# Turning the first rows at full depth, and ScalarE as the issuer of three of the last stores

## The chip, the cores and the metric

The kernel runs on one core of one Trainium2 chip. The metric is device time in microseconds (us), the median of several executions. A core has five engines with an instruction stream each: PE (TensorE, matrix products), DVE (VectorE), ACT (ScalarE), POOL (GpSimd) and SP (SyncE, which here only issues DMAs). Engines wait for each other through semaphores. Sixteen DMA engines move data between the chip's main memory (HBM) and the on-chip memory SBUF; results of PE land in PSUM, eight banks that DVE and ACT read.

## The reference

Attention with a few extra keys in front, then a gated feed-forward network, all in float32 outside:

```
B, H, S, Nb, D = 8, 8, 576, 16, 64        # batches, heads, rows, beacon keys, head size
k_all = concat(beacon_k, k);  v_all = concat(beacon_v, v)          # 592 keys
scores = q @ k_all.T / 8;  causal mask on the 576 keys, beacons always seen
a = softmax(scores);  attn = a @ v_all                             # (8, 8, 576, 64)
x = attn with heads side by side                                   # (4608, 512)
out = (relu(x @ w_gate) * (x @ w_val)) @ w_out                     # 512 -> 1536 -> 512
```

The output is 4608 x 512 float32.

## The kernel before

**The work.** Attention goes batch by batch. For each batch, `new_batch` loads q, k and v with DMAs on SP into staging tiles `st` (seven of 128 x 512 float32), rounds them to bfloat16 tiles `h16` (three buffers `cast_s`; the function `rounded`, line 486, on POOL and for some of batch 0 on DVE), and turns them on PE: `turned` (line 490) multiplies the rounded rows with an identity matrix, so that head dimension comes to the partitions. There are ten turns per batch, of four matmuls each: four for k and four for q (128 rows, `load_pair`), and two from `load_rest`. Of these, "first" ("F" in the orders of loading) holds 48 rows of q and 16 beacon keys, 64 rows in all, and "last" ("L") holds 64 rows of k and 16 of q, 80 rows. In a turn, `h16` is the stationary operand (loaded into PE as weights) and the identity the moving one; the number of partitions that both take is the depth of the multiplication. DVE and ACT copy what was turned from PSUM to `kT` (keys) and `diag` (queries, block-diagonal for two heads). Then follow scores on PE (lines 655 to 663), masking and row minimum on DVE (678), the exponential on ACT (689), normalisation on POOL (710), transposes of the probabilities by DMA (by PE in batch 0), and the product with v on PE (766 and 795), which gives `xT`.

**The feed-forward part.** `hidden` forms gate and value products for up to 512 rows of `xT` at a time (line 833), with relu on ACT (837) and the product of both on DVE (841). `project` multiplies 128 rows with w_out (line 853), copies the result to one of four tiles `osb` on ACT or DVE, and stores it with a DMA on SP (line 865). Of each batch, 512 rows are done so. The last 64 rows of each batch are gathered over four batches, 256 rows at a time, so that a tile of 128 rows belongs to two batches and takes two stores of 64 rows. The second gathering (batches 4 to 7) is the last work of the kernel: one tile with 512 columns, then one tile in two halves of 256 columns (`LAST_PARTS`). That makes six stores of 64 rows at the very end.

**What sets the order.** All work is first given to `Plan` as tasks with an engine (or a choice of engines), a cost, dependencies, buffers and a priority. `Plan.order` simulates the engines with these costs and writes out one order of tasks; the instructions are emitted in it and each engine's stream is fixed by it. A "DMA" task is an issue on SP. A task that has "ACT" as its engine stands in ACT's stream among the copies and activations there. PE's stream mixes attention of coming batches with feed-forward work of earlier ones, so that feed-forward matmuls fill PE while the softmax of another batch is under way.

Of the kernel before, what the change touches and what calls it, by code (L numbers as in the profile page):

```python
# [51 lines left out]
OUT = -1300.0  # L52
# [93 lines left out]
class Plan:  # L146
# [7 lines left out]
    def add(self, engines, cost, run, deps=(), holds=(), prio=0.0, lag=None, part=False, lazy=0.0, after=0.0, move=0.0):  # L154
        t = Task(engines if isinstance(engines, tuple) else (engines,), cost, run, deps, holds, prio, lag, part, lazy, move)
        t.ready = after
        for d in t.deps:
            d.users.append(t)
        self.tasks.append(t)
        return t  # L160
# [107 lines left out]
def kernel(  # L268
# [12 lines left out]
    nc = tc.nc  # L281
    B, H, S, D = q.shape
# [4 lines left out]
    P = 128  # L287
# [31 lines left out]
    ident = cp.tile([P, P], BF16, name="ident")  # L319
# [33 lines left out]
    add = plan.add  # L353


    def c_dve(n):
        return 0.07 + 0.00104 * n
# [7 lines left out]
    def c_act(n):  # L365
        return 0.06 + 0.00083 * n
# [4 lines left out]
    def c_pe(n):  # L371
        return 0.003 + n / 2400.0
# [63 lines left out]
    def copy(e, dst, src):  # L436
        if e == "ACT":
            nc.scalar.copy(dst, src)  # L438
        elif e == "DVE":
            nc.vector.tensor_copy(dst, src)  # L440
        else:
            nc.gpsimd.tensor_scalar(dst, src, 1.0, 1.0, ALU.mult, ALU.mult)
# [25 lines left out]
    def new_batch(b, prio, work):  # L468
# [20 lines left out]

        def turned(h16, rows, ca, prio, users):  # L490
            ps = Hold(first_ps if b == 0 else v_ps, 1 + users)

            def turn(_):
                for a in range(4):

                    to = ps.tile[:, a * P:a * P + rows]
                    nc.tensor.matmul(to, h16.tile[:rows, a * P:(a + 1) * P], ident[:rows, :rows],  # L497
                                     start=True, stop=True)

            return ps, add("PE", c_pe(4 * rows), turn, (ca, on_ident), (h16, ps), prio[1])  # L500
# [13 lines left out]
        def load_pair(kind, p, prio):  # L514
# [12 lines left out]
            halves = 1 if kind == "k" else 2  # L527
            zeros = on_zeros.get(b) if kind == "q" else None
            ps, tu = turned(h16, P, ca, prio, halves)

            def evict(x):
# [18 lines left out]
        def load_rest(kind, prio):  # L550
# [15 lines left out]
            i = 0 if kind == "first" else 1  # L566
            h16, ca = rounded((t.kT, t.diag), st, rows, scales[:rows, i:i + 1], prio, ld, lambda t_: t_)
            ps, tu = turned(h16, rows, ca, prio, 3)

            def evict_k(x):  # L570
# [251 lines left out]
    def hidden(rhs, w, c0, deps, hT, prio):  # L822
        hid = []
        for nf in range(NF):
            psg, psv, g = Hold(f_s, 2), Hold(f_s, 2), Hold(gate_s, 2)

            def product(w_r, ps, nf=nf):
                for ki in range(KM):
                    x = rhs(ki)
                    to = ps.tile[:, :w]  # L830
                    if len(x.shape) == 3:
                        to = to.rearrange("p (b s) -> p b s", b=x.shape[1])
                    nc.tensor.matmul(to, w_r[:, ki, nf * P:(nf + 1) * P], x, start=(ki == 0), stop=(ki == KM - 1))  # L833

            a = add("PE", 4 * c_pe(w), lambda _, f=product, ps=psg: f(wg_r, ps), deps + [weight_in["g", nf // 4]],
                    (psg,), prio + 0.02 * nf)
            r = add("ACT", c_act(w), lambda _, psg=psg, g=g: nc.scalar.activation(  # L837
                g.tile[:, :w], psg.tile[:, :w], AF.Relu), (a,), (psg, g), -1000 + prio)
            b_ = add("PE", 4 * c_pe(w), lambda _, f=product, ps=psv: f(wv_r, ps), [a, weight_in["v", nf // 4]],
                     (psv,), prio + 0.02 * nf + 0.01)  # L840
            hid.append(add("DVE", c_dve(w), lambda _, psv=psv, g=g, nf=nf: nc.vector.tensor_mul(  # L841
                hT[nf].tile[:, c0:c0 + w], g.tile[:, :w], psv.tile[:, :w]), (r, b_), (psv, g, hT[nf]), -1000 + prio))
        return hid

    def project(t0, rows, here, hT, prio, last):
        w = DM // LAST_PARTS if last else DM
        for n0 in range(0, DM, w):
            ps, osb = Hold(f_s, 4), Hold(osb_s, 1 + len(rows))
            prev = None
            for part in range(3):  # L850
                def outp(_, part=part, ps=ps, n0=n0):
                    for nf in range(4 * part, 4 * part + 4):
                        nc.tensor.matmul(ps.tile[:, :w], hT[nf].tile[:, t0:t0 + P], wo_r[:, nf, n0:n0 + w],  # L853
                                         start=(nf == 0), stop=(nf == NF - 1))

                need = [prev, weight_in["o", part]]
                for hid in here:
                    need += hid[4 * part:4 * part + 4] + (hid[:11] if part == 0 else [])
                prev = add("PE", 4 * c_pe(w), outp, need, (ps,) + tuple(hT[4 * part:4 * part + 4]),
                           prio + 0.3 + 0.01 * part + 0.001 * (n0 > 0) - (0.5 if part else 0))  # L860
            ev = add(("ACT", "DVE"), {"ACT": c_act(w), "DVE": c_dve(w)}, lambda x, ps=ps, osb=osb: copy(
                x.engine, osb.tile[:, :w], ps.tile[:, :w]), (prev,), (ps, osb), -1000 + prio)
            at = 0
            for r0, n in rows:
                add("DMA", (0.4, 0.78 * n / P), lambda _, osb=osb, r0=r0, n=n, at=at, n0=n0: nc.sync.dma_start(
                    out[r0:r0 + n, n0:n0 + w], osb.tile[at:at + n, :w]), (ev,), (osb,), prio + OUT)
                at += n


# [13 lines left out]
    def done(b, lo, hi):  # L883
        return [x for (b0, what, _), x in x_done.items() if b0 == b and SPAN[what][0] < hi and SPAN[what][1] > lo]

    REG = S // MT * MT
    for b in range(B):
        hT = [Hold(hid_s, len(CUTS.get(b, ())) + 1 + REG // P) for _ in range(NF)]
        cuts = [0, *CUTS.get(b, ()), REG]
        prio = 1000 + 10.0 * b  # L890
        here = []
        for a, z in zip(cuts, cuts[1:]):
            here.append(hidden(lambda ki, a=a, z=z, b=b: xT[:, ki, b * S + a:b * S + z], z - a, a, done(b, a, z), hT, prio))
            for t0 in range(a // P * P, z // P * P, P):
                project(t0, [(b * S + t0, P)], [x for x, c0, c1 in zip(here, cuts, cuts[1:]) if c0 < t0 + P and c1 > t0],
                        hT, prio, False)
            prio += 2.0
    ends = xT.rearrange("p k (b s) -> p k b s", s=S)
    for i in range(2):
        b0, b1 = i * B // 2, (i + 1) * B // 2  # L900
        w = (b1 - b0) * (S - REG)
        prio = 1000 + 10.0 * b1 - 5.0
        hT = [Hold(hid_s, 1 + w // P + (LAST_PARTS - 1) * i) for _ in range(NF)]
        deps = [x for b in range(b0, b1) for x in done(b, REG, S)]
        hid = hidden(lambda ki, b0=b0, b1=b1: ends[:, ki, b0:b1, REG:], w, 0, deps, hT, prio)
        for t0 in range(0, w, P):
            b = b0 + t0 // (S - REG)
            project(t0, [(x * S + REG, S - REG) for x in (b, b + 1)], [hid], hT, prio, i == 1 and t0 + P == w)

    def fill(n, to):  # L910
        for _ in range(n):
# [34 lines left out]
```

## Time and profile before

| | us |
|---|---|
| median of 3 runs | 409.17 (408.51 to 409.42) |
| the profiled execution | 410.43 |
| its span, first to last instruction | 408.7 |
| PE busy | 394.1 (96%) |
| DVE busy | 315.8 (77%) |
| ACT busy | 289.9 (71%) |
| POOL busy | 232.7 (57%) |
| granted PE clock, mean | 0.997 |

The profile is of one execution. Its page gives the busy time of each engine, the span in 40 slices of 10.2 us (each digit is a busy share in tenths), and the chain of work that ended last, followed back from the last instruction. From the trace behind it one can list waits by engine, and the timeline of a stretch: start, length, engine, line, operation, and the tiles written and read; consecutive instructions of one group are merged, and "x4" tells how many. "PEld" is the loading of weights into PE, which overlaps matmuls; "SPq" is the issuing of DMAs on SP. A matmul's form such as "64*128 64x64" names first the part of the array that the weights occupy (rows * columns) and then the moving operand. Durations of matmuls overlap their neighbours, so the room that one takes on PE is read from start to start.

### The profile page before, as it was taken

The page shows a single profiled execution, that of the slowest core. Times are in us where ns is not written, and L with a number is a line of the kernel's source. Part 1 is how long each engine was busy: PE and PEld are TensorE (multiplying, and loading weights), DVE is VectorE, ACT ScalarE, POOL GpSimd, SP SyncE. Part 2 cuts the span into 40 slices and gives each one's busy share as a digit, 9 for nine tenths or more (in the row PEclk, how much of TensorE's full clock was granted, in tenths as well). Part 3 has the DMA queues.
Part 4 walks back from the last instruction along what each step waited for, and adds up shares of the span by engine and source line. Part 5 has one row for each costly group of instructions (what it writes and reads, how often), then busy time and mean ns, then how long its engine had stood idle before and what let it go on. Part 6 is the DMA issues. An engine that isn't in the chain of part 4 may idle for free.

```text
span 408.7 us, 10376 instructions
## 1 busy us (share of the span) xinstructions
PE 394.1 (96%) x3276; PEld 246.8 (60%) x3311; DVE 315.8 (77%) x1159; ACT 289.9 (71%) x959; POOL 232.7 (57%) x434
## 2 busy tenths in 40 slices
PE   7899999989999999999999999999999999999994
PEld 5567867567766877555557754654554544444483
DVE  6898999889989988899998998787988544244251
ACT  6899989778888968797888799998867432033040
POOL 5899786947777667586975966875727200000000
PEclk9999999999999999999999999999999999999998
DMA  8899999999989999999999999999195730100112
GB/s 224 167 199 225 212 209 196 171 242 219 176 172 230 215 178 231 190 227 195 242 209 210 234 198 189 249 201 205 54 162 125 167 73 0 70 34 0 53 54 51
DMA packets 172616, 68.03 MB, mean 166 GB/s; under 512 B 146832, under 2 KB 168080, under 8 KB 172560
## 3 DMA queue, kind: packets, MB, share of 16 engines
q1 hardware_dynamic: 167808, 62.64, 75.5%
q0 software_dynamic: 4752, 4.72, 7.1%
q8 instruction: 26, 0.43, 0.5%
q14 instruction: 30, 0.25, 0.2%
HBM read 38.27 MB, written 9.44 MB: 117 GB/s over the span
## 4 chain that ended last, share of the span: by engine, by line
PE 84%; POOL 7%; DMA 2%; DVE 2%; ACT 2%; issue 2%; SPq 0%; POOLq 0%
PE f L833 42%; PE f L853 22%; PE f L663 7%; PE f L766 5%; PE f L497 4%; POOL xT L710 2%; POOL pb L710 2%; POOL h L486 2%; PE f L655 2%; DMA st<-in_beacon_k_dram 1%; PE f L795 1%; DMA st<-in_q_dram 1%; DVE diag L440 1%; PE f L745 1%; ACT xT L689 1%
## 5 line engine op out<-in xcount | busy, mean ns | idle before, releaser
L710 POOL TENSOR_SCALAR pb<-pb,small 128x576 bf16<-128x576 bf16 (+8 forms) x224 | 121.6, 557 | 56.0 <-DVE small L703 49.0
L689 ACT ACTIVATE pb<-f,small 128x64 bf16<-128x64 f32 (+6 forms) x256 | 131.0, 524 | 18.0 <-DVE small L678 13.1
L837 ACT ACTIVATE g<-f 128x512 f32<-128x512 f32 (+3 forms) x156 | 71.9, 470 | 67.9 <-PE f L833 66.6
L678 DVE CUSTOM_DVE_ANT_0 f<-f,mask 128x128 f32<-128x128 f32 (+7 forms) x256 | 112.0, 477 | 9.4 <-PE f L663 7.2
L833 PE MATMUL f<-xT,wv_r 128*128 128x512 bf16 (+3 forms) x616 | 111.8, 313 | 0.5
L833 PE MATMUL f<-xT,wg_r 128*128 128x512 bf16 (+3 forms) x619 | 109.5, 313 | 0.3
L841 DVE TENSOR_TENSOR hT<-g,f 128x512 bf16<-128x512 f32 (+3 forms) x156 | 80.5, 520 | 37.6 <-PE f L833 34.4
L853 PE MATMUL f<-wo_r,hT 128*128 128x512 bf16 (+1 forms) x423 | 102.0, 373 | 1.0
L833 PEld LDWEIGHTS <-wg_r 128*128 128x128 bf16 x624 | 60.0, 98 | 32.3 <-issue 0.2
L833 PEld LDWEIGHTS <-wv_r 128*128 128x128 bf16 x624 | 59.4, 98 | 33.0 <-issue 0.8
L853 PEld LDWEIGHTS <-hT 128*128 128x128 bf16 x444 | 41.6, 98 | 39.1
L689 ACT ACTIVATION_READ_ACCUMULATOR pb<-f,small 128x1 f32 x256 | 53.8, 210 | 0.0
L663 PE MATMUL f<-kT,diag 128*128 128x384 bf16 (+7 forms) x255 | 46.9, 286 | 1.9 <-DVE diag L440 0.8
L678 DVE DVE_READ_ACCUMULATOR2_ANT small<- 128x1 f32 x296 | 41.6, 141 | 0.2 <-issue 0.2
L486 POOL TENSOR_SCALAR h<-st 128x512 bf16<-128x512 f32 x62 | 37.8, 614 | 7.1 <-DMA st<-in_q_dram 2.9
L440 DVE COPY osb<-f 128x512 f32<-128x512 f32 (+1 forms) x26 | 17.6, 678 | 23.2 <-PE f L853 22.7
L710 POOL TENSOR_SCALAR xT<-xT,small 128x64 bf16<-128x64 bf16 (+4 forms) x64 | 26.9, 436 | 7.7 <-ACT xT L689 4.1
L497 PE MATMUL f<-ident,h 128*128 128x128 bf16 (+2 forms) x320 | 28.1, 217 | 2.8 <-POOL h L486 2.5
L438 ACT CAST diag<-f 64x512 bf16<-64x512 f32 (+2 forms) x52 | 23.0, 442 | 9.6 <-PE f L497 4.1
L497 PEld LDWEIGHTS <-h 128*128 128x128 bf16 (+2 forms) x320 | 20.3, 98 | 15.6 <-POOL h L486 7.9
L440 DVE CAST diag<-f 64x512 bf16<-64x512 f32 (+2 forms) x44 | 26.3, 598 | 4.2 <-ACT diag L438 2.0
L663 PEld LDWEIGHTS <-diag 128*128 128x128 bf16 x256 | 20.4, 98 | 15.0 <-issue 1.5
(67 smaller groups left out, 376.7 us busy)
## 6 DMA issues: line engine op xcount, KB each, us to landing
st<-in_q_dram SPq DMA_DIRECT2D x32, 256.0 KB, 4.5
st<-in_k_dram SPq DMA_DIRECT2D x32, 256.0 KB, 5.0
out_dram<-osb SPq DMA_DIRECT2D x32, 256.0 KB, 2.6
st<-in_v_dram SPq DMA_DIRECT2D x24, 256.0 KB, 4.7
st<-in_v_dram SPq DMA_DIRECT2D x8, 224.0 KB, 4.9
wg_r<-in_moe_w_gate_dram POOLq DMA_DIRECT2D x3, 512.0 KB, 8.5
wv_r<-in_moe_w_val_dram POOLq DMA_DIRECT2D x3, 512.0 KB, 10.3
wo_r<-in_moe_w_out_dram POOLq DMA_DIRECT2D x3, 512.0 KB, 14.2
```

What stands on the lines that cost most here:

```text
L438: nc.scalar.copy(dst, src)
L440: nc.vector.tensor_copy(dst, src)
L486: (nc.gpsimd if x.engine == "POOL" else nc.vector).tensor_scalar(to, of, by, 1.0, ALU.mult, ALU.mult)
L497: nc.tensor.matmul(to, h16.tile[:rows, a * P:(a + 1) * P], ident[:rows, :rows], start=True, stop=True)
L663: nc.tensor.matmul(view(i), t.diag.tile[:, p, j * P:j * P + P], kT[:, p, :n], start=True, stop=True)
L678: nc.vector.tensor_tensor_reduce(out=view(i), in0=view(i), in1=msk, scale=1.0, scalar=small["t"][:, 0:1] if name in "EF" else 3.0e38, op0= ...
L689: nc.scalar.activation(ph.tile.rearrange("p a n -> p (a n)")[:, a:a + n], view(i), AF.Exp, bias=small["t"][:, low:low + 1], scale=-1.0, ac ...
L710: (nc.gpsimd if x.engine == "POOL" else nc.vector).tensor_scalar(one, one, small["t"][:, 8 + i:9 + i], 1.0, ALU.mult, ALU.mult)
L833: nc.tensor.matmul(to, w_r[:, ki, nf * P:(nf + 1) * P], x, start=(ki == 0), stop=(ki == KM - 1))
L837: r = add("ACT", c_act(w), lambda _, psg=psg, g=g: nc.scalar.activation(g.tile[:, :w], psg.tile[:, :w], AF.Relu), (a,), (psg, g), -1000 + ...
L841: hid.append(add("DVE", c_dve(w), lambda _, psv=psv, g=g, nf=nf: nc.vector.tensor_mul(hT[nf].tile[:, c0:c0 + w], g.tile[:, :w], psv.tile[: ...
L853: nc.tensor.matmul(ps.tile[:, :w], hT[nf].tile[:, t0:t0 + P], wo_r[:, nf, n0:n0 + w], start=(nf == 0), stop=(nf == NF - 1))
```

## The change

Two edits.

1. `turned` gives the four matmuls of a turn the full 128 partitions as depth, in every batch but the first, also when only 64 or 80 rows are wanted. The further rows of `h16` hold older values; the identity has zeros where they would count, and the output keeps its 64 or 80 columns.
2. In `project`, for the second gathering only (`final`), the second of the two stores of a tile is a task of ACT, which issues the DMA on its own queue. The first remains on SP. Of the last six stores, three are then issued by each.

The order of the instructions on PE, DVE and POOL and all their waits stay as they were. SP has three stores less at its end, ACT three more at its end, behind its last copy.

```diff
         def turned(h16, rows, ca, prio, users):
             ps = Hold(first_ps if b == 0 else v_ps, 1 + users)
+            deep = P if b else rows
 
             def turn(_):
                 for a in range(4):
 
                     to = ps.tile[:, a * P:a * P + rows]
-                    nc.tensor.matmul(to, h16.tile[:rows, a * P:(a + 1) * P], ident[:rows, :rows],
+                    nc.tensor.matmul(to, h16.tile[:deep, a * P:(a + 1) * P], ident[:deep, :rows],
                                      start=True, stop=True)
...
-    def project(t0, rows, here, hT, prio, last):
+    def project(t0, rows, here, hT, prio, last, final):
...
             for r0, n in rows:
-                add("DMA", (0.4, 0.78 * n / P), lambda _, osb=osb, r0=r0, n=n, at=at, n0=n0: nc.sync.dma_start(
-                    out[r0:r0 + n, n0:n0 + w], osb.tile[at:at + n, :w]), (ev,), (osb,), prio + OUT)
+                def store(x, osb=osb, r0=r0, n=n, at=at, n0=n0):
+                    (nc.scalar if x.engine == "ACT" else nc.sync).dma_start(out[r0:r0 + n, n0:n0 + w], osb.tile[at:at + n, :w])
+
+                if final and at:
+                    add("ACT", 0.6, store, (ev,), (osb,), prio + OUT)
+                else:
+                    add("DMA", (0.4, 0.78 * n / P), store, (ev,), (osb,), prio + OUT)
                 at += n
...
-            project(t0, [(x * S + REG, S - REG) for x in (b, b + 1)], [hid], hT, prio, i == 1 and t0 + P == w)
+            project(t0, [(x * S + REG, S - REG) for x in (b, b + 1)], [hid], hT, prio, i == 1 and t0 + P == w, i == 1)
```

More of the change, by code (lines that the diff above doesn't have):

```diff
@@ L895 @@
                 project(t0, [(b * S + t0, P)], [x for x, c0, c1 in zip(here, cuts, cuts[1:]) if c0 < t0 + P and c1 > t0],
-                        hT, prio, False)
+                        hT, prio, False, False)
             prio += 2.0
```

## The prediction

> **What bounds the kernel now.** I read the page's shares and slices first, then the chain that ended last.
>
> ```profile
> span 408.7 us, 10376 instructions
> PE 394.1 (96%) x3276; PEld 246.8 (60%) x3311; DVE 315.8 (77%) x1159; ACT 289.9 (71%) x959; POOL 232.7 (57%) x434
> PE   7899999989999999999999999999999999999994
> DMA  8899999999989999999999999999195730100112
> PE 84%; POOL 7%; DMA 2%; DVE 2%; ACT 2%; issue 2%; SPq 0%; POOLq 0%
> ```
>
> TensorE is nearly full from slice 2 to slice 39 and carries 84% of the chain; POOL carries 7%. So TensorE time saved counts, unless PE then arrives at something that POOL delivers. The list of PE's waits answers where that happens: between 36 and 125 us it has one line, and between 125 and 403.3 us none at all.
>
> ```profile
> PE f L497 <- POOL h L486: 2.3, 5, 0.7
> ```
>
> Next I read the timeline of PE around a turn of 64 rows (121 us, batch 3), one of 64 rows behind 128 rows (196 us, batch 5) and one of 80 rows behind 128 rows (189.8 us), and POOL's timeline at 121 us.
>
> ```profile
> 121.08 0.38 PE L853 MATMUL f<-wo_r,hT 128*128 128x512 bf16 x1
> 121.39 0.29 PE L497 MATMUL f<-ident,h 64*128 64x64 bf16 x4
> 121.61 1.04 PE L853 MATMUL f<-wo_r,hT 128*128 128x512 bf16 x4
> 122.59 0.40 PE L497 MATMUL f<-ident,h 128*128 128x128 bf16 x4
> 122.82 0.25 PE L663 MATMUL f<-kT,diag 128*128 128x64 bf16 x2
> ...
> 196.28 0.61 PE L497 MATMUL f<-ident,h 128*128 128x128 bf16 x8
> 196.82 0.60 PE L833 MATMUL f<-xT,wv_r 128*128 128x512 bf16 x2
> ...
> 189.78 0.53 PE L497 MATMUL f<-ident,h 128*128 128x128 bf16 x8
> 190.15 0.60 PE L833 MATMUL f<-xT,wv_r 128*128 128x512 bf16 x2
> ...
> 121.92 0.61 POOL L486 TENSOR_SCALAR h<-st 128x512 bf16<-128x512 f32 x1
> ```
>
> Starts tell more than durations here, since matmuls overlap: 121.39 − 121.08 is the room that one matmul took. Last comes the tail, in the timeline from 395 us and in the landings of the final stores.
>
> ```profile
> 401.51 0.69 DVE L440 COPY osb<-f 128x512 f32<-128x512 f32 x1 [2.97 <-PE f L853]
> 401.95 0.37 ACT L438 COPY osb<-f 128x256 f32<-128x256 f32 x1 [3.95 <-PE f L853]
> 402.23 3.71 SPq L865 DMA_DIRECT2D out_dram<-osb  x6
> 403.26 0.42 DVE L440 COPY osb<-f 128x256 f32<-128x256 f32 x1 [1.05 <-PE f L853]
> ...
> DMA to landing us min/median/max: 2.0/2.0/2.0
> ```
>
> The last result is in SBUF at 403.68, but SP works through six stores without a break from 402.23 to 405.94. The last one starts at 405.35 and lands 2.0 later at 407.4, 1.47 after its issue ends; 1.3 of closing steps follow.
>
> **The change, part 1: full depth in the turn.** It alters four matmuls for "F" (64 rows) and four for "L" (80 rows) in each of batches 1 to 7; batch 0 stays. No instruction is added, and the order on PE and every wait are the same.
>
> What 64 rows cost now. Four matmuls of 128 columns take 122.82 − 122.59 = 0.23, so 0.057 each, and by columns 0.029 for one of 64. A 512-column matmul takes about 0.216 (the 49 in a run at 356.29 take 10.74). At 121 us, the way in is 0.31 − 0.216 = 0.09 too long, and four matmuls to the next start take 0.22 where 4 × 0.029 = 0.12 would do: 0.10 on the way out. Together 0.19, with some 0.01 on the next matmul 0.20. The two pairs check it: 4 × 0.057 + 4 × 0.029 = 0.34, taken 0.54 with 64 rows: 0.20 lost. With 80 rows 4 × 0.057 + 4 × 0.036 = 0.37, taken 0.37: nothing lost. So the 80-row half of the edit is worth 0, and a 64-row visit loses 0.20. At full depth the 64 columns should keep 0.029: bounds are 0.029 and the 0.057 of the 128-column form (+0.11 a visit), and I take the first, because even 32-column matmuls at 128 rows (L795, 14 from 231.03 to 231.46) start 0.031 apart.
>
> The Trainium skill ("TensorEngine Tiling (Array Packing)", Key Properties) says that a change of tiling mode drains the array; its Performance Considerations advise 2x row tiling for a contract dimension up to 64, which speaks against this change. By the advice the narrow form would gain up to half of 0.12 per visit; the trace shows no such gain, only the 0.20 of going in and out, so by it the sum would be higher by at most 7 × 0.06 = 0.4.
>
> What reaches the end. Batch 1 (38.6 us) and batch 2 (79.1 us): the way in hides under a wait for POOL's cast (both are among the five waits above), and what the way out frees is eaten by the later waits of that list (87.7 and 91.1 us, 0.6 and 0.7 long). Batch 3: at 122.59 PE starts 0.06 after POOL's cast ended (121.92 + 0.61), and the four L853 matmuls before it were done issuing at 121.61 + 0.88 = 122.49, so PE already waits 0.10; arriving earlier gains nothing unless POOL is earlier too. Batches 4 to 7 (164.1, 196.6, 232.6, 267.5 us) meet no wait that shows: 4 × 0.20 = 0.80. Bounds: 0 if casts or scores turn out only just in time, 7 × 0.20 = 1.4 if all comes through. From 300 us only PE is busy, on feed-forward matmuls whose inputs are long ready, so what is saved by then is kept.
>
> **Part 2: ScalarE issues three of the last six stores**, the second of each pair. They stand on ACT's queue behind its last copy (done 402.32), and nothing stands behind them, so they delay no compute; on SP, the first store of the next pair moves up. SP's stores now take 0.55 to 0.59 each. After: SP starts at 402.23, about 402.8, and the third when DVE's copy is done, 403.71 (the first one started 0.03 after its copy). ACT starts at about 402.35 and 402.95, and its third at 403.71 too. Landing 2.05 after: 405.76 instead of 407.40, so 1.64 less. Two stores of 64 KB now come at once; the slice 404 to 405 us moved 198 GB/s, so one may delay the other by up to 0.33. I take 0.09: 1.55.
>
> An ACT-issued store is not in this trace. The nearest rows are SP's own stores on line 865, 0.33 to 1.08 us an issue; that an engine's first DMA costs more is not to be seen on SP, whose first two, at 0.80 us, took 0.97 together. With x an issue, ACT's third ends at 402.45 + 3x and lands 1.47 later. x = 0.33 gives the same 1.64, since the third waits for the copy; x = 1.08 lands at 407.16: 0.24 gained. I take 0.6, the last stores being the nearest, and keep 0.2 and 1.65 as ends.
>
> **Sum.** 410.43 (profiled execution: span 408.7 and 1.7 around it) − 0.80 − 1.55 = 408.08. The median of the runs, 409.17, is 1.26 below that execution; so 406.8 as a median.
>
> **Rivals.**
> - *Part 1 is swallowed, part 2 holds.* between 121 and 197 us DVE works 90% and POOL 72% of the time, and the DMA engines are full to about 270 us; a cast that ends only 0.15 us ahead of its turn (the turns at 190.0 and 226.4 us) can take back what was won. Against it: no wait at all after 125 us. 409.17 − 1.55 = 407.6.
> - *Part 1 comes through in all seven batches*: 409.17 − 1.4 − 1.55 = 406.2. For it: POOL's casts partly follow PE; against it: the five waits.
> - *ACT issues at SP's slowest, 1.08*: 409.17 − 0.80 − 0.24 = 408.1.
> - *The other side: ACT's issue is slow beyond SP's rows.* Place: three issues in a row on ACT from 402.35. Part 2 gains nothing from x = 1.16 ((407.40 − 1.47 − 402.45) / 3), and the kernel is slower by over 0.82 from x = 1.70 (3x has then grown by 0.80 + 0.82 more). At x = 2.0 the landing is at 409.9: 409.17 + 2.5 − 0.8 = 410.9. Against it: SP's longest store is 1.08, and that in a full DMA stretch.
> - *Full-depth weight loads can't hide.* A load takes 98 ns; exposed, 28 of them cost 2.7: 409.17 + 2.7 − 0.80 − 1.55 = 409.5. Against it: full-depth loads with 128 columns already start 0.057 apart. The Trainium skill ("TensorE: Matmul & The Clock Gate", Part 3, What overlaps and what doesn't) says that loads overlap running matmuls only in another row group; these rows contradict that here.
> - *The edit does not do what it says for time* (the closing steps wait for something else): 409.2. The landing at 407.4 and the closing steps right behind speak against it.
>
> **How the numbers follow.** Forecast 0.46; part 1 swallowed 0.22; all seven batches 0.12; ACT at 1.08 0.09; ACT slower than 1.70 0.06; loads exposed 0.03; no effect 0.02. The forecast's value is 406.8. The range runs from 405.9 (all seven batches, and 0.3 for the spread of medians) to 408.4 (ACT at 1.08, same allowance); outside remain the last three cases, 0.11, and tails of the others. A measurement can tell about 0.2%, 0.82 us. Faster by more: 0.46 + 0.22 + 0.12 and half of 0.09, 0.84; within: the rest of that and most of loads exposed and no effect, 0.09; slower: ACT slower than 1.70 and a tail of loads exposed, 0.07.
>
> **What would show it.** Right, if in batches 4 to 7 the F turn reads 128*128 with 128x64 and the next matmul starts about 0.34 instead of 0.54 after the start of the 128 rows; if the last copy still ends about 0.8 earlier than 403.68; if the two last stores start together within 0.1 of that copy's end and the span ends some 3.5 after it instead of 5.0. Part 1 is wrong if new PE waits for POOL or DVE appear between 164 and 300 us that add up to 0.8; part 2 if ACT's issues last over 1 us each or the stores land later than 2.4 after their start.

## The result and the profile after

| | before | after |
|---|---|---|
| median, us | 409.33 (408.51 to 411.04, 6 runs) | 406.82 (406.16 to 407.43, 6 runs) |
| the profiled execution | 410.43 | 407.43 |
| its span | 408.7 | 405.6 |
| from the end of the last copy to the end of the span | 5.04 | 3.39 |

The ratio is 0.9931 with a 95% interval of 0.991 to 0.9952: faster by 0.7%, 2.5 us. The same pair, measured twice more in the experiments below, gave 0.9921 (0.9895 to 0.9946) and 0.9935 (0.9914 to 0.9956). Two executions in the experiments, one of 2057.63 us (part 1 alone) and one of 458.06 us at a granted clock of 0.852 (part 2 alone, the profiled one, of which only the tail is read), count in the medians but not in the ratios.

The page of after has the same picture as before, with the code lines behind each edit moved down by one or two (the turn is now L498, `hidden` L834, `project` L854, its stores L867):

```profile
span 405.6 us, 10379 instructions
PE 393.0 (97%) x3276; PEld 246.9 (61%) x3311; DVE 314.6 (78%) x1159; ACT 289.8 (71%) x959; POOL 232.6 (57%) x434
...
PE 85%; POOL 6%; ACT 2%; DMA 2%; DVE 2%; issue 1%; SPq 0%; POOLq 0%; ACTq 0%; DVEq 0%
```

TensorE is still the bound. The groups of the turn, kept apart by shape (busy time, mean ns of one, then the idle time before them and its releaser), show that the edit is in force: 28 matmuls with 64 columns and 28 with 80 now read 128*128, and only batch 0's are short.

```profile
L498 PE MATMUL f<-ident,h 128*128 128x128 bf16 x256 | 24.3, 222 | 0.8 <-POOL h L486 0.6
L498 PE MATMUL f<-ident,h 128*128 128x80 bf16 x28 | 2.2, 202 | 1.0 <-POOL h L486 1.0
L498 PE MATMUL f<-ident,h 128*128 128x64 bf16 x28 | 2.0, 194 | 0.3 <-POOL h L486 0.2
L498 PE MATMUL f<-ident,h 64*128 64x64 bf16 x4 | 0.3, 219 | 0.0
L498 PE MATMUL f<-ident,h 80*128 80x80 bf16 x4 | 0.3, 205 | 0.0
```

The first turn of batch 5, 64 rows behind 128 rows, in PE's timeline of after:

```profile
195.21 0.50 PE L498 MATMUL f<-ident,h 128*128 128x128 bf16 x8
195.55 0.81 PE L834 MATMUL f<-xT,wv_r 128*128 128x512 bf16 x3
```

195.55 − 195.21 = 0.34 where the same pair took 0.54 before. Last, the tail:

```profile
400.08 0.69 DVE L440 COPY osb<-f 128x512 f32<-128x512 f32 x1 [2.97 <-PE f L854]
400.51 0.37 ACT L438 COPY osb<-f 128x256 f32<-128x256 f32 x1 [3.95 <-PE f L854]
400.79 1.95 SPq L867 DMA_DIRECT2D out_dram<-osb  x3
400.80 2.07 ACTq L867 DMA_DIRECT2D out_dram<-osb  x3
401.82 0.42 DVE L440 COPY osb<-f 128x256 f32<-128x256 f32 x1 [1.05 <-PE f L854]
```

SP and ACT issue three stores each, side by side. The last copy ends at 402.24, and both third stores start right behind it, at 402.27 on SP and 402.32 on ACT. The span ends at 405.63, 3.39 after the copy.

### The profile page after: what moved, and what is told of

It reads as the page before. It is cut to its first block, busy times and chain, and to the rows that moved or that the text cites. A ratio compares the mean times of both kernels' runs of the same rounds, so it can differ in the third digit from the quotient of the medians.

```text
span 405.6 us, 10379 instructions
## 1 busy us (share of the span) xinstructions
PE 393.0 (97%) x3276; PEld 246.9 (61%) x3311; DVE 314.6 (78%) x1159; ACT 289.8 (71%) x959; POOL 232.6 (57%) x434
## 4 chain that ended last, share of the span: by engine, by line
PE 85%; POOL 6%; ACT 2%; DMA 2%; DVE 2%; issue 1%; SPq 0%; POOLq 0%; ACTq 0%; DVEq 0%
PE f L834 43%; PE f L854 22%; PE f L664 7%; PE f L767 5%; PE f L498 4%; POOL xT L711 2%; DMA st<-in_q_dram 2%; PE f L656 2%; POOL pb L711 1%; PE f L796 1%; POOL h L486 1%; PE f L746 1%; DVE diag L440 1%; PE f L659 1%; ACT xT L690 1%
## 5 line engine op out<-in xcount | busy, mean ns | idle before, releaser
L834 PE MATMUL f<-xT,wv_r 128*128 128x512 bf16 (+3 forms) x616 | 111.8, 313 | 0.6
L834 PE MATMUL f<-xT,wg_r 128*128 128x512 bf16 (+3 forms) x619 | 109.5, 313 | 0.3
L854 PE MATMUL f<-wo_r,hT 128*128 128x512 bf16 (+1 forms) x423 | 101.9, 373 | 1.0
L834 PEld LDWEIGHTS <-wg_r 128*128 128x128 bf16 x624 | 60.0, 98 | 32.3 <-issue 0.2
L834 PEld LDWEIGHTS <-wv_r 128*128 128x128 bf16 x624 | 59.4, 98 | 32.9 <-issue 0.8
L854 PEld LDWEIGHTS <-hT 128*128 128x128 bf16 x444 | 41.6, 98 | 38.9
L498 PE MATMUL f<-ident,h 128*128 128x128 bf16 (+3 forms) x320 | 28.0, 218 | 2.1 <-POOL h L486 1.8
L498 PEld LDWEIGHTS <-h 128*128 128x128 bf16 (+1 forms) x320 | 20.9, 99 | 13.9 <-POOL h L486 6.7
```

The costliest lines, as they stand in the source:

```text
L498: nc.tensor.matmul(to, h16.tile[:deep, a * P:(a + 1) * P], ident[:deep, :rows], start=True, stop=True)
```

## The experiments

All medians are compared with runs of the kernel before on the same chip. The diffs stand against the changed kernel.

### Each part alone, and the kernel before against itself

The changed kernel once more, part 1 alone, part 2 alone, and the kernel before under another name. The edit for part 1 alone, which gives all six stores back to SP:

```diff
-                if final and at:
+                if False and final and at:
```

> The full depth alone; all six last stores stay on SP. The recorded theory: four visits of 64 rows (batches 4 to 7) give 0.20 each and all of it reaches the end: 0.8 us below the kernel before, and from the last copy's end to the span's end 5.0 as before. Rival, from the profile of the changed kernel, where a new wait of 1.0 us for POOL's cast stands at 188.9: what is won up to batch 4 is swallowed there, so only batches 5 to 7 count, 0.6 us or less. Second rival, all seven batches: 1.4 us. In the trace every one of the seven visits is 0.19 to 0.20 shorter in all three.

The edit for part 2 alone:

```diff
-            deep = P if b else rows
+            deep = rows
```

> Three stores on ACT alone; the turns keep their 64 and 80 rows. The recorded theory: 1.55 us below the kernel before (bounds 0.2 and 1.65); the profile of the changed kernel showed 3.4 from the end of the last copy to the end of the span, against 5.0 before, so 1.6 here too if the parts are independent. PE's starts as in the kernel before, within what two executions of it differ by. Rival: the stores on ACT owe part of their gain to the other part, then less than 1.2.

> The changed kernel once more. If the parts add: the gains of the two runs before it together, 2.4 by the recorded theory, 2.2 or less by the rival that swallows batch 4's. The waits of PE for POOL's casts at 87, 91 and 189 us tell whether these belong to the kernel or to one execution: the theory that they belong to the change expects the one at 189 again and those at 87 and 91 gone; the theory of chance expects another pattern.

> The kernel before against itself: ratio 1.000, and its interval says what five rounds can tell. Its trace is a second look at PE's waits: if those of 0.6 and 0.7 us at 87.7 and 91.1 belong to the kernel, they are there again and none stands after 125 us; if they are chance, both differ.

Later, on another chip, part 1 alone and the changed kernel were measured a second time:

> The full depth alone, once more, since its first interval (0.9965 to 1.001) did not tell 0.8 us from nothing. From the pair of traces with the same waits before 100 us (kernel before, second look, against this kernel): PE's lead grows by 0.2 at each visit of batches 3 to 7, loses 0.27 at two new waits, and is 0.8 at the end. Together with the first: 0.4 to 1.0 us below the kernel before.

> The changed kernel beside the three that follow, so that they are compared on one chip. As before: 0.992 of the kernel before, 3.4 from the end of the last copy to the end of the span, two waits of PE of 0.14 and 0.13 at about 234 and 268 us that the kernel before has not.

| kernel | median, us | kernel before, us | ratio (95% interval) | last copy to end of span |
|---|---|---|---|---|
| before against itself | 409.41 | 408.96 | 0.9998 (0.9973 to 1.0023) | 5.05 |
| part 1 alone | 408.54 | 408.96 | 0.9988 (0.9965 to 1.001) | 5.06 |
| part 1 alone, again | 408.2 | 408.85 | 0.9994 (0.9976 to 1.0013) | 5.05 |
| part 2 alone | 407.5 | 408.96 | 0.9956 (0.9934 to 0.9978) | 3.36 |
| both | 406.43 | 408.96 | 0.9921 (0.9895 to 0.9946) | 3.37 |
| both, again | 406.24 | 408.85 | 0.9935 (0.9914 to 0.9956) | 3.40 |

Part 2 alone took 1.46 off the median, and the tail in its trace is shorter by 1.68 than in the first profile; over the six rows the tail has just two lengths, 5.05 and 3.38, with no more than 0.02 to either side. Part 1 alone took 0.42 and 0.65 off the medians; neither interval leaves out "no change". That it is worth something therefore had to come from the traces and from the next experiments. On the medians the two parts alone add up to 1.88 to 2.11, and both together gave 2.53 and 2.61; with intervals of 0.7 to 1.0 us to either side, these medians don't show whether the parts help each other.

**What the second profile of the kernel before says.** It has the same instructions as the first and a span of 407.0 instead of 408.7. PE's waits from 36 to 125 us, which were "2.3, 5, 0.7" (total, times, longest) in the first profile, are here:

```profile
PE f L497 <- POOL h L486: 1.0, 2, 0.8
```

Two of the waits that the prediction took for lasting, at 87.7 and 91.1 us, are gone, and with them 1.6 us: the lead of this execution grows by 0.72 and 0.88 there. In the first one POOL's casts had been late at these places. Waits of this kind come and go by execution. The profile of after has one that no other look at this kernel has at that length, at 188.93 us:

```profile
188.19 0.69 POOL L486 TENSOR_SCALAR h<-st,scales 80x512 bf16<-80x512 f32 x1 [1.40 <-DMA st<-in_q_dram]
188.93 0.32 PE L498 MATMUL f<-ident,h 128*128 128x80 bf16 x4 [0.98 <-POOL h L486]
```

The cast waited 1.40 us for a load, and PE 0.98 for the cast. In the two other traces of the changed kernel, PE's list of waits between 125 and 403 us is empty. So single profiles of this kernel can't be subtracted from each other without first looking at which of these waits each one has.

**Part 1, place by place.** The second profile of before and part 1 alone happen to have much the same early waits (two each between 36 and 125 us), and comparing the start of each matmul in the two gives how far ahead the changed one is:

| place | part 1 alone | part 1 alone, again |
|---|---|---|
| lead just before the 64 rows of batch 3 | 0.17 | 0.17 |
| each turn of 64 rows in batches 3, 4, 5, 6 and 7 | +0.19 to +0.21 | +0.19 to +0.21 |
| turns of 80 rows | 0 | 0 |
| the turn of 128 rows behind batch 3's 64 rows | 0 | −0.05 |
| about 234.6 us, a turn of 128 rows | −0.14 | −0.14 |
| about 268.2 us, scores | −0.13 | −0.14 |
| lead at the end | 0.96 | 0.90 |

In batches 1 and 2 the lead of 0.1 to 0.2 goes again at the next matmuls that POOL releases (40.2, 42.0 and 79.7 us). Net, part 1 is worth 0.79 and 0.73. PE's timeline at batch 3, the kernel before (second profile):

```profile
118.80 1.03 PE L853 MATMUL f<-wo_r,hT 128*128 128x512 bf16 x4
119.76 0.29 PE L497 MATMUL f<-ident,h 64*128 64x64 bf16 x4
119.98 1.04 PE L853 MATMUL f<-wo_r,hT 128*128 128x512 bf16 x4
120.86 0.39 PE L497 MATMUL f<-ident,h 128*128 128x128 bf16 x4
```

and part 1 alone:

```profile
118.63 1.03 PE L854 MATMUL f<-wo_r,hT 128*128 128x512 bf16 x4
119.50 0.28 PE L498 MATMUL f<-ident,h 128*128 128x64 bf16 x4
119.61 1.03 PE L854 MATMUL f<-wo_r,hT 128*128 128x512 bf16 x4
120.47 0.39 PE L498 MATMUL f<-ident,h 128*128 128x128 bf16 x4
```

The way into the turn takes 0.87 instead of 0.96, the way through it 0.11 instead of 0.22, and the lead of 0.17 becomes 0.26, 0.37 and 0.39. The turn of 128 rows behind it, which the prediction took to be held by POOL, follows at once in both: four matmuls later, 0.88 and 0.86.

That isn't so in every execution. Of the ten traces of kernels that have full depth in batch 3, five start this turn 0.86 to 0.87 after the matmuls ahead of it. The other five start it 0.05 to 0.06 after the end of POOL's cast, and so 0.05 to 0.32 later behind those matmuls than the first five. The profile of after is one of these, with 1.01:

```profile
119.54 1.03 PE L854 MATMUL f<-wo_r,hT 128*128 128x512 bf16 x4
119.88 0.61 POOL L486 TENSOR_SCALAR h<-st 128x512 bf16<-128x512 f32 x1
120.55 0.34 PE L498 MATMUL f<-ident,h 128*128 128x128 bf16 x3
```

The first repetition of the changed kernel waits longest, 0.32, and the second one not at all. So batch 3's visit is a gain in some executions and is taken back, wholly or in part, in others.

The loss at 234 us, again before (second profile) and part 1 alone:

```profile
233.11 1.39 DVE L440 CAST diag<-f 64x512 bf16<-64x512 f32 x2
...
234.33 0.46 PE L663 MATMUL f<-kT,diag 128*128 128x320 bf16 x2
...
234.63 0.39 PE L497 MATMUL f<-ident,h 128*128 128x128 bf16 x4
```

```profile
232.31 1.39 DVE L440 CAST diag<-f 64x512 bf16<-64x512 f32 x2
...
233.31 0.46 PE L664 MATMUL f<-kT,diag 128*128 128x320 bf16 x2
...
233.75 0.38 PE L498 MATMUL f<-ident,h 128*128 128x128 bf16 x4
```

PE's scores come 1.02 earlier, DVE's copies of the turns before only 0.80. Before, the turn of 128 rows began 0.13 after the copies' end; now it begins 0.05 after it, and 0.44 instead of 0.30 after the start of the scores. Of the 0.22 that PE won beyond what DVE won, 0.08 uses up the slack between them, and 0.14 is taken back here. The wait is too short to stand in the list of waits. That the turn waits for a PSUM bank which these copies free is the reading of the trace's semaphore events; no run took the copies away. At 268 us the same is read with ACT's exponential in place of the copies: it ended at 268.04 and the scores began at 268.17 before, 0.13 later; with part 1 alone it ended at 267.16 and they began at 267.21, 0.05 later.

### The cost of a change of depth, put back where it counts and where it does not

On the changed kernel, matmuls 0 and 2 of the two short turns are given a depth of 64 and matmuls 1 and 3 keep 128. Each such turn then goes in and out twice, so batches 4 to 7 hold 16 visits to the short form instead of the 4 of the kernel before, and batches 1 to 3 hold 12. A depth of 64 leaves 16 rows of q out of the 80-row turns, so these two kernels serve for their times alone. The edit for batches 4 to 7 (for 1 to 3, `0 < b < 4`):

```diff
-            deep = P if b else rows
...
+                    deep = 64 if rows < P and a % 2 == 0 and (b > 3) else P if b else rows
```

> On the changed kernel: in batches 4 to 7, of the four matmuls of both short turns (64 and 80 rows) the first and third have a depth of 64, the others 128. That makes four visits to the 64-row form in a batch, 16 in all, where the changed kernel has none. (With a depth of 64 the turn of 80 rows leaves out 16 rows of q in two of four matmuls.) Theory: a visit costs PE 0.2 wherever it stands, and in batches 4 to 7 PE's time is the kernel's: 16 x 0.2 = 3.2 above the changed kernel, less at most 0.3, since the two waits of 0.14 and 0.13 that the changed kernel has at 234 and 268 us go away again. Rival, POOL and DVE set the pace there and PE has room: less than 1.0.

> The same in batches 1 to 3: 12 visits. If a visit costs the same wherever it stands: 12 x 0.2 = 2.4 above the changed kernel. By the recorded theory PE waits for POOL's casts there and the way in is hidden and the rest eaten: nothing, at most 0.4. By what two pairs of traces showed since (batch 3's visit went through in one of them): 0.4 to 1.0, from batch 3's four visits.

Measured: 409.45 against 408.75, ratio 1.0019 (1.0001 to 1.0037), for batches 4 to 7; 407.38, ratio 0.9973 (0.9963 to 0.9984), for batches 1 to 3. The changed kernel stood 2.51 to 2.61 below the kernel before, these two stand 0.70 above and 1.37 below it. So 16 late visits cost 3.2 to 3.3 us, 0.20 each, as expected, and 12 early ones 1.1 to 1.2, a little above the 0.4 to 1.0 expected. In the trace of the early one, batch 3's four visits take 0.83 and reach the end; the eight of batches 1 and 2 go almost wholly into the waits for POOL's casts. PE's timeline at the turn of batch 5 with two visits:

```profile
195.64 0.92 PE L498 MATMUL f<-ident,h 128*128 128x128 bf16 x8
196.40 1.89 PE L834 MATMUL f<-xT,wv_r 128*128 128x512 bf16 x8
```

0.76 from the turn of 128 rows to the next matmul, where the changed kernel took 0.34: 0.21 a visit. In this kernel, in which the late visits are back, the two losses at 234 and 268 us turn into gains of the same size against the changed kernel (0.14 and 0.13). That ties these waits to PE's being ahead of DVE and ACT.

### All six stores on ScalarE

```diff
-                if final and at:
+                if final:
```

> On the changed kernel: ACT issues all six last stores, SP none of them. It measures an issue on ACT by six in a row without SP's beside them. Theory: ACT's issue costs what SP's does, 0.55 to 0.6 each, so the end of the last copy to the end of the span is 5.0 again, as in the kernel before, and the time lies 1.6 above the changed kernel. Rival: ACT's issue is dearer by itself (one of its three took 0.77 in the changed kernel): at 0.77 each, 6.0 to 6.2 and 2.7 above the changed kernel.

Measured: 408.14 against 408.75, ratio 0.9985 (0.9973 to 0.9996), tail 5.15. The times of ACT's issues (min/median/max in ns), and the tail's timeline:

```profile
L867 ACTq DMA_DIRECT2D out_dram<-osb x6: 552/577/617, 399.5 to 402.7; - x6
```

```profile
399.48 3.79 ACTq L867 DMA_DIRECT2D out_dram<-osb  x6
400.51 0.42 DVE L440 COPY osb<-f 128x256 f32<-128x256 f32 x1 [1.05 <-PE f L854]
```

ACT alone issues a 64-row store in 0.55 to 0.62, about as SP does (0.51 to 0.60). Six in a row on it end at 403.27, long after the last copy (400.93), and the tail is about as long as with six on SP. So what part 2 gains is two queues in place of one, not ScalarE in place of SyncE. As the tail here is 0.1 longer than before's, the gain of this kernel, 0.61, is part 1's, and it is the one run of part 1 without part 2 whose interval leaves out "no change".

### One store of 128 rows for each pair

If issuing is what the tail waits for, half as many stores should do it too. The two stores of a tile become one, whose target has the two batches as its outer dimension:

```diff
+            if final:
+                both = out.rearrange("(b s) n -> b s n", s=S)[rows[0][0] // S:rows[0][0] // S + 2, REG:S, n0:n0 + w]
+                add("DMA", (0.4, 0.78), lambda _, osb=osb, both=both: nc.sync.dma_start(
+                    both, osb.tile[:, :w]), (ev,), (osb,), prio + OUT)
-            for r0, n in rows:
+            for r0, n in rows if not final else []:
```

> On the changed kernel: each pair of last stores is one DMA of 128 rows on SP (its target has two blocks of 64 rows), three issues in all, none on ACT. If it is the queue of issues that cost the 1.6, this gains as much as the second issuer: 3.4 from the end of the last copy to the end of the span, and by the 128-row stores of the quiet stretch (0.33 an issue, against 0.55 for 64 rows) 0.1 to 0.2 less than that. Rival, the second queue itself is what helps (two queues land sooner): above 3.6.

Measured: 415.94 against 408.75, ratio 1.0184 (1.0163 to 1.0204), tail 13.08. The gain that was expected failed to come, and while the tail is above the 3.6 of the rival, it isn't for the rival's reason. SP's issues, and a stretch of 2 us after the last copy (stretch, length, busy time of PE, PEld, DVE, ACT and POOL, granted clock, DMA share, GB/s):

```profile
L867 SPq DMA_DIRECT2D out_dram<-osb x3: 522/653/3604, 399.7 to 401.2; - x3
```

```profile
404.00:406.00 2.00, 0.00 (x0) 0.00 (x0) 0.00 (x0) 0.00 (x0) 0.00 (x0) 0.50 0.13 49
```

Two of the three issues are as short as hoped. But with nothing else under way the transfers use 0.13 of the sixteen DMA engines, two of them, and move 50 GB/s; the changed kernel's tail moves 252 GB/s between 402 and 404 us. The third issue then takes 3.6 us. The Trainium skill ("DMA: Bandwidth & Descriptors", Why a DMA increments its semaphore by 16 and not by 1) says that a DMA uses the largest number of engines, up to 16, that divides the slowest dimension of both its sides; with an outer dimension of 2 that is 2, and the share of 0.13 agrees.

To test this, the same one store was given a target whose outer dimension is 32. That needs the rows of the gathered tile in the order row by row, four batches each, which the second gathering's products write into PSUM in steps of four elements:

```diff
-                        to = to.rearrange("p (b s) -> p b s", b=x.shape[1])
+                        to = to.rearrange("p (s b) -> p b s" if sb else "p (b s) -> p b s", b=x.shape[1])
...
+                b0, s0 = rows[0][0] // S // 4 * 4, REG + t0 // 4
+                both = out.rearrange("(b s) n -> s b n", s=S)[s0:s0 + 32, b0:b0 + 4, n0:n0 + w]
```

> On the changed kernel: the last gathering orders its 256 rows by row and then by batch, so that one store of 128 rows has a target of 32 x 4 rows instead of 2 x 64; three stores, all on SP, none on ACT. Theory from the run with 2 x 64 (moved 48 GB/s, a share of 0.13 to 0.14 of the 16 DMA engines, so two of them): the outer dimension of 2 was what cost 9 us, not the merging; with 32 it goes to all engines, lands about 2 after its start, and the end of the last copy to the end of the span is 3.2 to 3.5. Rival: a target of more than one dimension is slow as such: well above 5. The 128x256 products of the last gathering write PSUM in steps of 4; if that costs PE time, their spacing shows it (0.109 now).

Measured: 416.37 against 408.85, ratio 1.0186 (1.016 to 1.0212). The tail is the shortest of all, 3.13, and at 410 to 412 us the DMA engines are used again:

```profile
410.00:412.00 2.00, 0.26 (x3) 0.00 (x0) 0.42 (x1) 0.00 (x0) 0.00 (x0) 1.00 0.57 203
```

So the outer dimension was the cause of the slow landing. What this kernel lost lies elsewhere, in the products of the second gathering. Its PE timeline, and the same products of the changed kernel:

```profile
396.21 1.93 PE L834 MATMUL f<-xT,wg_r 128*128 128x256 bf16 x8
397.94 1.93 PE L834 MATMUL f<-xT,wv_r 128*128 128x256 bf16 x8
```

```profile
390.30 1.04 PE L834 MATMUL f<-xT,wg_r 128*128 128x256 bf16 x8
391.17 1.04 PE L834 MATMUL f<-xT,wv_r 128*128 128x256 bf16 x8
```

Eight take 1.73 from start to start instead of 0.87: 0.216 each instead of 0.109. There are 96 of them, so this costs about 96 × 0.107 = 10.3. Permuting what the products read, instead of what they write, wasn't tried.

### Another cut of the last tile

The halves of 256 columns become 384 and 128, so that the last copy and the last stores are smaller:

```diff
-        w = DM // LAST_PARTS if last else DM
-        for n0 in range(0, DM, w):
+        for n0, w in ((0, 384), (384, 128)) if last else ((0, DM),):
```

> On the changed kernel: the last tile is cut into 384 and 128 columns instead of 256 and 256, so that the very last copy and stores are half as large; DVE makes both copies. If the end is a chain of PE, last copy, issue and landing: the last copy takes 0.29 instead of 0.42 and the rest stays, 0.1 to 0.2 less from PE's last matmul to the end of the span (3.8 now). Rival: an issue on SP and ACT is still under way for the 384 columns when the last copy ends (each takes 0.55, and DVE's copy of 384 ends about 0.6 before that of 128); then nothing is gained, or up to 0.2 is lost.

Measured: 407.03 against 408.85, ratio 0.9954 (0.9937 to 0.997), beside 406.24 for the changed kernel on the same chip. From the start of the last matmul to the end of the span it takes 4.62, the changed kernel 4.13. That is 0.49 more, where 0.1 to 0.2 less was expected and the rival allowed for 0.2 more. Its timeline:

```profile
401.91 1.19 SPq L866 DMA_DIRECT2D out_dram<-osb  x2
401.91 0.29 DVE L440 COPY osb<-f 128x128 f32<-128x128 f32 x1
401.96 1.44 ACTq L866 DMA_DIRECT2D out_dram<-osb  x2
```

The last copy ends at 402.20, but ACT's second issue, begun at 401.96, lasts 0.79, and its third store starts at 402.84. In the changed kernel the third stores started 0.03 and 0.08 after the last copy. An even cut leaves just the time that two issues need; the shorter last part gives it up. No kernel tried was faster than the changed one.

## Why the prediction was right, and where it was not

The median, 406.82, is the 406.8 that was forecast, but not every term was right.

**Part 2: right, 0.1 too small.** Forecast 1.55, measured 1.65 in the pair of first profiles and 1.68 with part 2 alone. The guess of 0.6 for an issue by ACT was near: ACT's first and third took 0.555 and 0.553 in the changed kernel, and all six on ACT 0.55 to 0.62. ACT's second issue in the changed kernel took 0.773. It cost nothing, as the copy came later still. The two last stores landed at 404.29 and 404.48, 2.02 and 2.16 after their start. The later one took 0.11 more than the 2.05 of the kernel before (0.09 was taken); the last of six on ACT took 2.09, so not all of that has to come of two at once. The last landing comes 2.24 after the copy instead of 3.71, which is 1.47 of the gain. The other 0.18 is the term that was missed: the closing steps behind the last landing were taken as a fixed 1.3. They take 1.33 to 1.34 in every trace with six stores on one queue, be it SP's or ACT's, 1.10 to 1.18 with three on each of two, and 1.02 to 1.03 with three stores in all. The rivals that ACT issues at 1.08, or slower than 1.70, and that the closing steps wait for something else, are out.

**Part 1: the size near, its make-up wrong.** Forecast 4 × 0.20 = 0.80; the two traces show 0.79 and 0.73, and the medians 0.42 and 0.65, with intervals that reach from a loss of 0.5 to a gain of 1.4. Right were the 0.20 of a visit, by the timelines and by the visits that were put back; the 0 for the turns of 80 rows; and the loads: with 64 columns a turn takes 0.11 to 0.12 at full depth, so loads of 98 ns hide, and the rival of exposed loads is out.

The step that failed is "Batch 3: ... arriving earlier gains nothing unless POOL is earlier too". It made a rule of a wait of 0.10 in one execution. In the second profile of before the four matmuls ahead of the turn of 128 rows take 0.88 and not 0.98, so there was nothing to be held by, and with part 1 alone batch 3's 0.20 comes through, whole in one trace and less 0.05 in the other. Where POOL's cast is later the step holds, as in five of the ten traces above. Against this gain stand two losses that the prediction left out of its sum, 0.14 and 0.13, where PE gets ahead of DVE's copies and ACT's exponential. 5 × 0.205 − 0.27 = 0.75. So the 0.80 came out by two errors that cancel, which is luck; with the hold behind batch 3, of 0.05 to 0.32, the same sum gives 0.70 to 0.43. The rival "swallowed" looked for late casts and had all of the 0.80 taken back; what was taken back for good is a third of that, and by the copies and the exponential. "All seven batches" was wrong about batches 1 and 2, whose visits are covered by waits in every pair of traces compared.

By its letter one of the prediction's own signs against part 1 came up: new waits of PE for POOL between 164 and 300 us that add up to 0.8. The profile of after has 0.98 at 188.93 us. As told above, a late load made it, and the two repetitions of the changed kernel don't have it.

**The test by the end of the last copy** was met for another reason. It was to end 0.8 earlier than 403.68 and ended at 402.24, 1.44 earlier. In these two profiles the lead is 0.28 before 87.7 us and grows by 1.6 at the two waits that the profile of before has and that of after has not, and by 1.0 at the five turns; it loses 0.05 behind batch 3, 0.27 at the two known places, and 1.15 at 188.93 us, by the wait of 0.98 there and the time that it took to start again. The sum was made against the profiled execution and then moved to the median by 1.26; that step is why the long waits of that one execution did little harm to the forecast. The prediction counted them as lasting, though, and gave them two batches to swallow; the same two batches are covered in the quieter profile as well, by the waits at 40.2, 42.0 and 79.7 us.

How much of the last 0.2 between traces and medians (0.75 + 1.66 = 2.41 against 2.51 to 2.61) is anything but the spread of runs stays open.

## What to carry to other kernels

Look at what the last result waits for after it has been computed: when several small stores stand in one queue behind the last copy, sharing them between two idle queues takes the queue out of the path, and a cut of the last tile is good when each queue's issues are done just as the next copy ends. A matmul of short depth among full-depth ones can cost more in going in and out than it saves, so multiplying padding with zeros can be the cheaper form. Before a wait in one profile is used as a cover or as a gain, look whether a second profile of the same kernel has it.

## What the runs showed of the hardware beyond what was expected

- A change between a depth of 64 and 128 rows costs 0.09 to 0.11 us each way here, whether a visit holds four matmuls or one. A depth of 80 costs nothing of the kind.
- A store whose target has an outer dimension of 2 ran on two of sixteen DMA engines: 50 GB/s, and landings 2.7 us apart for 128 KB. With 32 as the outer dimension the last store of the same rows landed 2.07 after its start. The DMA share of the stretch shows it, and the distance of the landings.
- Matmuls of 256 columns that write float32 to PSUM in steps of four elements take twice the room, 0.216 instead of 0.109. The Trainium skill ("SBUF — State Buffer", Door 1: The DMA port swizzle, in its note on cachelines) says that PSUM has 8-byte cachelines and that a non-contiguous PSUM access slows matmuls significantly; the trace agrees, and puts the factor at 2.0 for this step.
- The closing steps after the last landing differ with the last stores: 1.02 to 1.03 us with three on one queue, 1.10 to 1.18 with three on each of two, 1.33 to 1.34 with six on one. What they consist of, and whether the stores or the queues count, no trace shows.
- ACT's second issue of three lasted 0.77 to 0.79 us where SP issued beside it (in every trace of this sort, the changed kernel's and the uneven cut's among them), against 0.55 to 0.62 for all six with SP silent. Since the first and third of those three took 0.50 to 0.56 with SP beside them too, the cause stays open.
- The Trainium skill ("DMA: Bandwidth & Descriptors", Issuing engines are not separate DMA queues) says that issuing from several engines saves only the sequencer's time, usually small beside the DMA. The runs agree with the first half for 1.47 of the 1.65 us that a second queue took off a tail of 5.04; the other 0.18 came in the closing steps. Small it wasn't here.
